# A hand-ordered mixer network: the same instructions in a new order, from a planner with another rule for GpSimd's single-column work

## The chip, the cores and the metric

The kernel runs on one core of one Trainium2 chip, as one program. The metric is the device time of that program in microseconds; the time before is the median of three runs. A core has TensorE (PE, matmuls into PSUM), VectorE (DVE), ScalarE (ACT), GpSimd (POOL) and SyncE (SP, which here only issues DMAs). Each engine works through its own instruction list strictly in order, and waits on semaphores for what other engines make.

## The reference

Two layers with shared weights, on x of 2048 rows and 512 columns in float32. Each layer is an attention A with a window of 8 keys at distance 2, and a mixer B:

```python
x = x + _A_ref(_layernorm(x), A_wqkv, A_wo)
x = x + _B_ref(_layernorm(x), B_w1, B_w2, B_w3, B_w4)
# and both once more

def _A_ref(x, wqkv, wo):            # 32 heads of 16, W = 8 keys at offsets 0, 2, .., 14 back
    q, k, v = split(x @ wqkv)
    logits = einsum("bhsd,bhswd->bhsw", q, k_window) * 16 ** -0.5
    logits = where(position >= 0, logits, -1e9)
    o = einsum("bhsw,bhswd->bhsd", softmax(logits), v_window)
    return o @ wo

def _B_ref(x, w1, w2, w3, w4):      # w1, w2: 512x512; w3: 512x1792; w4: 1792x512
    h = gelu(_layernorm(x) @ w1)
    hs = concatenate(h's four quarters of columns, shifted by +1, -1, +2, -2 rows) @ w2
    x1 = x + hs
    return x1 + gelu(_layernorm(x1) @ w3) @ w4
```

## The kernel before

Tiles are of 128 rows. A block is 512 rows (four tiles), and the two layers make eight blocks, numbered 0 to 7 (0 to 3 are the first layer's). A block goes through five stages: p1 (layernorm, x @ wqkv, results to DRAM), p2 (attention, read back from DRAM so that a window lies in one partition), p3 (wo, layernorm, w1, Gelu, shifted copies), p4 (w2, residual, layernorm) and p5 (w3, Gelu, w4, residual, in 14 chunks of 128 hidden columns). Stages of different blocks overlap freely.

A float32 product is made from fp16 pieces: each operand is scaled and split in a high and a low part, and three matmuls of 512 columns replace one. A group of 12 matmuls (4 row blocks times 3) is the usual unit on TensorE. Block 0 uses float32 matmuls, since its weights are not yet split; the splitting of the weights (`small_weight` for wo, w1, w2 and `big_pair` for chunks of w3 and w4: a Square with a running sum on ScalarE, a one-column matmul with `ones` that sums over partitions, a power on GpSimd, then the high and low parts) runs beside the first blocks.

What the engines do around the matmuls:

- ScalarE evicts PSUM, does Gelu and the exponential (two function tables, ACT_TABLE_LOAD between them), the Square sums of layernorm (`junk<-`), the normalizations and the high parts.
- VectorE does the attention: products of 128x2048 elements (`prod<-kv,q`, `prod<-kv,L`), their sums (`L<-prod`, `prod<-prod`, `o<-prod`), and low parts (SCALAR_TENSOR_TENSOR, TENSOR_TENSOR subtractions) and residual additions.
- GpSimd does the column work of layernorm, `power`: three instructions on single columns of the tile `small` (scale and add, power -0.5, the shift), written `small<-small`. It also takes some of VectorE's and ScalarE's wide work and the small shifted copies `h<-h` in p3.
- SyncE issues DMAs, the transposing ones too (`xt<-f`, `nT<-f`, `oT<-f`), which turn a normalized tile for the next matmul.

The order is not the program's. Each step is recorded as an operation with its alternatives (engine, expected duration, function), its reads and writes, and a place in one global order, from the table `PLACES`; the table `OTHER` names the operations that take their second alternative, another engine. `plan` sorts by place, hands out buffers of each kind (x, f32, mm for PSUM and so on) by its own expected times, and issues; a helper, `InOrder`, keeps every engine to that order. All instructions are issued through the helper, so the profile puts them all on line 338 (347 after the change), and they are told apart by their tiles. Where names differ between the two orders (`nT_168`, `nT_170`; `prod_206`, `prod_203`), they are buffers' numbers. Four buffers of 512 columns are quarters of the tile `prod0`, so a normalized tile can bear the name `prod`.

In the planner's model an operation has a class: "lock" is a VectorE instruction with two operands in SBUF, which shares a port with GpSimd. Before the change every GpSimd operation and every lock operation waits in the model for the one before it:

```python
if e == POOL or cls == "lock":
    begin = max(begin, port)
    port = begin + d
```

The steps that the prediction speaks of are `power` and `power_of` (columns), `sq_dev` (Square sums), `normed` (normalization), `turn_dma` (transposing DMA), `hi_of` and `rest` (parts of weights), the copies in `p3`, and the stages that call them.

Of the kernel before, what the change touches and what calls it, by code (L numbers as in the profile page):

```python
# [218 lines left out]
class Graph:  # L219
# [3 lines left out]
    def __call__(self, key, alts, r=(), w=(), after=(), xfer=0.0, late=0.0):  # L223
# [34 lines left out]
        return o  # L258


LAT, LAT_PE, LAT_SP, LAT_DMA, LEAD, TABLE, COLD = 0.06, 0.4, 0.15, 1.5, 0.85, 1.3, 1.0
TAIL = (0.165, 0.085, 0.115, 0.0, 0.0)
FREE = (6.5, 1.0, 0.72, 1.2, 0.72)
LANES = 8
BY_DMA = {"p1": 1, "p2": 1, "p3": 1, "p4": 1}


def plan(ops, slots):


    free, latest = list(FREE), {}
# [1163 lines left out]
```

## Time and profile before

| | |
|---|---|
| median of three runs | 1144.0 us |
| lowest and highest run | 1142.68 and 1894.58 us |
| the profiled execution | 1145.03 us |
| its span, first to last instruction | 1143.2 us |
| busy: TensorE / VectorE / ScalarE / GpSimd | 98% / 75% / 54% / 37% |
| granted TensorE clock, mean | 0.997 |
| moved by DMA | 206.37 MB, 181 GB/s |

One of the three runs took 1894.58 us, far from the other two. "Busy" counts an engine's own work; TensorE's weight loads (PEld) overlap its matmuls. A group's row ends with busy time, mean duration of one in ns, and the idle time just before its instructions with what ended it. An "issue" is time without a wait that the profile shows.

### The profile page before, as it was taken

To read this page: it belongs to the slowest core of one execution; us is meant where nothing else is said; L and a number is where in the kernel's file an instruction comes from. 1 tells how busy PE (TensorE), PEld (TensorE's weight loads), DVE (VectorE), ACT (ScalarE), POOL (GpSimd) and SP (SyncE) were. 2 spreads that over 40 slices of the span, in tenths; PEclk is the share of its full clock that TensorE was granted. 3 is DMA by queue.
4 is the path that set the end of the run, shared out by engine and by line. 5 is a ranking of instruction groups with operands and counts; after the bars stand their busy time and mean duration, and the time that the engine had idled before them with its cause. 6 is when DMAs were issued, how large, how long until landed. Compare 5 with 4: busy or idle time off the path is not lost.

```text
span 1143.2 us, 15112 instructions
## 1 busy us (share of the span) xinstructions
PE 1124.1 (98%) x5190; PEld 532.4 (47%) x5190; DVE 862.6 (75%) x919; ACT 618.6 (54%) x1089; POOL 417.9 (37%) x596
## 2 busy tenths in 40 slices
PE   8989999999999999999999999999999999999998
PEld 6544445554444444444444444444444444444554
DVE  4989899997899998988888888378986888323212
ACT  4766785247863565464654565354555554535321
POOL 4342364125652571135534353252324342322000
PEclk9999999999999999999999999999999999999999
DMA  6988989997989669974679756596687865524322
GB/s 175 217 205 215 223 216 259 256 238 182 265 234 222 162 161 211 244 187 121 161 182 230 192 136 166 128 237 177 154 206 166 199 168 158 113 75 112 100 88 79
DMA packets 249165, 206.37 MB, mean 181 GB/s; under 512 B 131032, under 2 KB 192472, under 8 KB 249088
## 3 DMA queue, kind: packets, MB, share of 16 engines
q1 hardware_dynamic: 247472, 203.63, 72.3%
q10 hardware_dynamic: 1616, 1.77, 0.5%
q8 instruction: 41, 0.67, 0.2%
q14 instruction: 36, 0.29, 0.1%
HBM read 132.64 MB, written 37.87 MB: 149 GB/s over the span
## 4 chain that ended last, share of the span: by engine, by line
PE 60%; ACT 2%; DVE 1%; issue 1%; POOL 1%; POOLq 0%; DVEq 0%; ACTq 0%
PE mm L338 42%; PE acc L338 18%; POOL small L338 1%; ACT f L338 1%; DVE L L338 0%; DVE prod L338 0%; ACT junk L338 0%; DVE f L338 0%; ACT L338 0%; ACT g L338 0%; ACT mm L338 0%; POOL f L338 0%; DVE x L338 0%; POOL o L338 0%; DVE h L338 0%
## 5 line engine op out<-in xcount | busy, mean ns | idle before, releaser
L338 PE MATMUL acc<-w,g 128*128 128x512 f16 (+1 forms) x1260 | 307.3, 394 | 0.0
L338 PE MATMUL mm<-nT,w 128*128 128x512 f16 (+1 forms) x1288 | 301.7, 389 | 0.8 <-ACT f L338 0.8
L338 PE MATMUL mm<-wq_hl,xt 128*128 128x512 f16 x1008 | 226.8, 381 | 3.2 <-DMA xt<-f 2.3
L338 ACT ACTIVATE mm<-mm,s_w 128x512 f32<-128x512 f32 (+1 forms) x144 | 89.7, 628 | 195.0 <-PE mm L338 194.7
L338 PEld LDWEIGHTS <-w 128*128 128x128 f16 x1344 | 125.2, 98 | 142.2 <-issue 1.0
L338 PEld LDWEIGHTS <-g 128*128 128x128 f16 x1176 | 114.7, 98 | 137.5
L338 DVE TENSOR_TENSOR prod<-kv,L 128x2048 f32<-128x2048 f32 x64 | 148.7, 2325 | 13.6 <-POOL o L338 12.2
L338 PEld LDWEIGHTS <-xt 128*128 128x128 f16 x1008 | 98.8, 98 | 122.5 <-issue 4.8
L338 DVE TENSOR_REDUCE L<-prod 128x128 f32<-128x2048 f32 x64 | 146.2, 2284 | 1.2
L338 POOL TENSOR_SCALAR small<-small 128x1 f32<-128x1 f32 (+1 forms) x200 | 88.8, 444 | 137.8 <-ACT junk L338 123.8
L338 DVE TENSOR_TENSOR prod<-kv,q 128x2048 f32<-128x2048 f32 x58 | 134.3, 2316 | 3.7 <-DMA q<-q_d 1.9
L338 DVE TENSOR_TENSOR prod<-prod 128x512 f32<-128x512 f32 (+2 forms) x109 | 111.5, 1026 | 2.7
L338 POOL TENSOR_TENSOR g<-f,g 128x512 f16<-128x512 f32 x39 | 54.8, 1409 | 117.8 <-ACT g L338 69.2
L338 DVE SCALAR_TENSOR_TENSOR g<-mm,c_g,g 128x512 f16<-128x512 f32 x56 | 41.5, 745 | 63.7 <-ACT g L338 63.7
L338 PE MATMUL mm<-w_hl,h 128*128 128x512 f16 x384 | 85.7, 379 | 1.1 <-POOL h L338 1.1
L338 PE MATMUL mm<-nT,w_hl 128*128 128x512 f16 x384 | 86.5, 379 | 0.0
L338 POOL TENSOR_TENSOR small<-small,nhalf 128x1 f32<-128x1 f32 (+1 forms) x104 | 72.3, 695 | 8.7
L338 PE MATMUL mm<-wo_hl,oT 128*128 128x512 f16 x336 | 74.3, 379 | 0.0
L338 POOL TENSOR_TENSOR prod<-prod 128x512 f32<-128x512 f32 (+1 forms) x24 | 30.5, 1271 | 105.9 <-DVE prod L338 99.4
L338 ACT ACTIVATE ev<-mm,s_kv 128x512 f32<-128x512 f32 x56 | 38.1, 681 | 54.8 <-PE mm L338 40.0
L338 ACT ACTIVATE g<-mm,c_g 128x512 f16<-128x512 f32 x98 | 66.6, 684 | 1.9
L338 PEld LDWEIGHTS <-oT 128*128 128x128 f16 x426 | 41.5, 98 | 49.0 <-issue 0.6
(188 smaller groups left out, 1217.8 us busy)
## 6 DMA issues: line engine op xcount, KB each, us to landing
w<-w SPq DMA_DIRECT2D x196, 256.0 KB
kv<-kv_d SPq DMA_DIRECT2D x112, 352.0 KB
w<-in_B_w_dram SPq DMA_DIRECT2D x56, 256.0 KB
kv_d<-ev SPq DMA_DIRECT2D x112, 128.0 KB
q_d<-ev SPq DMA_DIRECT2D x28, 256.0 KB
w<-g SPq DMA_DIRECT2D x28, 256.0 KB
q<-q_d SPq DMA_DIRECT2D x28, 256.0 KB
x<-x SPq DMA_DIRECT2D x26, 256.0 KB
```

The source lines that it names most:

```text
L338: i = f(*a, **k).ins
```

## The change

The planner's model of the shared port changes, and with it the two tables. GpSimd's column operations (`power`, `power_of`'s power, and the four-column chain of p3) get the class "tiny". In the new model GpSimd still waits for a running lock operation, up to `GRANT` before its end; a lock operation waits only for wide GpSimd work (`wide`), not for tiny; and what needs a tiny operation's result waits another `HELD`. The latency to TensorE goes from 0.4 to 0.35, and some expected durations on GpSimd are new. The functions that make the instructions stay as they are; `PLACES` is another order, and `OTHER` moves some operations: GpSimd issues 36 instructions more, VectorE 12 and ScalarE 16 fewer (accumulator reads and the like not counted). TensorE's instructions are the same in number.

```diff
 PLACES = [int(k) for k in """
-15 29 72 33 3 148 0 1 6 5 19 12 8 13 7 21 40 58 20 45 2 4 14 16
+40 41 58 128 94 96 0 1 4 5 12 13 11 9 10 26 53 31 39 28 2 3 15 16
...
 OTHER = {int(k): 1 for k in """
-27 37 100 101 104 107 116 178 181 187 226 235 256 277 304 361 366 396 421 422 425 465 483 566
+27 32 37 102 103 106 114 118 120 126 140 158 177 178 181 183 187 201 205 225 228 229 231 232
...
-LAT, LAT_PE, LAT_SP, LAT_DMA, LEAD, TABLE, COLD = 0.06, 0.4, 0.15, 1.5, 0.85, 1.3, 1.0
+LAT, LAT_PE, LAT_SP, LAT_DMA, LEAD, TABLE, COLD = 0.06, 0.35, 0.15, 1.5, 0.85, 1.3, 1.0
 TAIL = (0.165, 0.085, 0.115, 0.0, 0.0)
 FREE = (6.5, 1.0, 0.72, 1.2, 0.72)
 LANES = 8
+GRANT, HELD = 0.14, 0.6
...
-    dma_free, port, table, order = 0.0, 0.0, None, []
+    dma_free, port, wide, table, order = 0.0, 0.0, 0.0, None, []
...
-            if e == POOL or cls == "lock":
-                begin = max(begin, port)
+            if e == POOL:
+                if begin < port:
+                    begin = max(begin, port - GRANT)
+                if cls != "tiny":
+                    wide = begin + d - GRANT
+            elif cls == "lock":
+                begin = max(begin, wide)
                 port = begin + d
             if e == PE and begin - free[PE] > COLD and begin > 20.0:
                 d += min(begin - free[PE] - COLD, 2.5)
             o.end = begin + d + (TAIL[PE] if e == PE else 0.0)
             free[e] = o.end - TAIL[e]
+            if cls == "tiny":
+                o.end += HELD
...
-    def gp(key, d, fn, r, w, after=()):
-        return op(key, [(POOL, d, fn, None)], r, w, after)
+    def gp(key, d, fn, r, w, after=(), cls=None):
+        return op(key, [(POOL, d, fn, cls)], r, w, after)
...
-        gp(key, 1.24, fn, [(ss, j), (tot, k)], [(ve, i), (r, i), (nb, i)])
+        gp(key, 1.24, fn, [(ss, j), (tot, k)], [(ve, i), (r, i), (nb, i)], cls="tiny")
```

Three places of the new order. The first is ScalarE at the Square of w2 (`w_hl,ss_w_152`), some 60 us in; `ev` are evictions of the first layer's qkv results for block 1. Before:

```order
L338 ACTIVATE wo_hl<-nT_200,inv_wo 128x1024
L338 ACTIVATE ev_208<-mm_66,s_kv 128x512
L338 ACTIVATE junk,ss_p_146<-w_188 128x512
L338 ACTIVATE junk,ss_p_146<-w_192 128x512
L338 ACTIVATE w_hl,ss_w_152<-nT_168 128x2048
L338 ACTIVATE ev_209<-mm_68,s_kv 128x512
L338 ACTIVATE ev_165<-mm_70,s_q 128x512
```

and now:

```order
L347 ACTIVATE wo_hl<-nT_195,inv_wo 128x1024
L347 ACTIVATE ev_208<-mm_70,s_kv 128x512
L347 ACTIVATE ev_209<-mm_66,s_q 128x512
L347 ACTIVATE w_hl,ss_w_152<-nT_170 128x2048
L347 ACTIVATE ev_194<-mm_68,s_kv 128x512
```

Two evictions stand ahead of the Square, where one stood, and two Squares of `big_pair` (`ss_p_146`) no longer stand between.

The second is ScalarE at the Squares of `big_pair` 1 (`ss_p_141`), some 279 us in; `f_182<-x_194` (before) and `f_198<-x_205` (now) are the normalization of a tile of block 4, which waits for GpSimd's columns. Before:

```order
L338 ACTIVATE junk,small<-x_194,small 128x512
L338 ACTIVATE junk,small<-x_185,small 128x512
L338 ACTIVATE junk,ss_p_141<-w_192 128x512
L338 ACTIVATE f_182<-x_194,small 128x512
L338 ACTIVATE junk,ss_p_141<-w_193 128x512
L338 ACTIVATE f_204<-f_182 128x512
```

and now:

```order
L347 ACTIVATE junk,small<-x_205,small 128x512
L347 ACTIVATE junk,small<-x_186,small 128x512
L347 ACTIVATE junk,ss_p_141<-w_184 128x512
L347 ACTIVATE junk,ss_p_141<-w_165 128x512
L347 ACTIVATE f_198<-x_205,small 128x512
L347 ACTIVATE prod_203<-f_198 128x512
```

Both Squares now stand ahead of the normalization.

The third is GpSimd some 540 us in, where block 3's shifted copies (`h_175<-h_184`, now `h_180<-h_181`) stand among p4's columns and wide work. Before:

```order
L338 TENSOR_SCALAR small<-small 128x1
L338 TENSOR_TENSOR small<-small,nhalf 128x1
L338 TENSOR_SCALAR small<-small 128x1
L338 MEMSET h_175 128x2x2
L338 TENSOR_TENSOR f_171<-f_173,f_171 128x512
L338 TENSOR_SCALAR f_204<-prod_206,small 128x512
L338 TENSOR_SCALAR small<-small 128x1
L338 TENSOR_TENSOR small<-small,nhalf 128x1
L338 TENSOR_SCALAR small<-small 128x1
L338 COPY h_175<-h_184 128x2
L338 COPY h_175<-h_184 128x2x2
```

and now:

```order
L347 COPY h_180<-h_181 128x2x2
L347 TENSOR_SCALAR small<-small 128x1
L347 TENSOR_TENSOR small<-small,nhalf 128x1
L347 TENSOR_SCALAR small<-small 128x1 x2
L347 TENSOR_TENSOR small<-small,nhalf 128x1
L347 TENSOR_SCALAR small<-small 128x1
L347 COPY h_180<-h_181 128x2
L347 TENSOR_TENSOR x_192<-x_192,prod_203 128x512
L347 TENSOR_TENSOR f_177<-f_168,f_177 128x512
```

One copy stands ahead of both column chains and one right behind them; the wide work follows.

More of the change, by code (lines that the diff above doesn't have):

```diff
@@ L556, in power_of @@
         p = inv.t[:, :m] if inv.kind is None and not isinstance(inv.t, tuple) else inv.t
-        gp(key, 1.03, lambda: G.tensor_tensor(p, f2.t[:, :m], nhalf[:, :m], ALU.pow), [f2], [inv])
+        gp(key, 1.03, lambda: G.tensor_tensor(p, f2.t[:, :m], nhalf[:, :m], ALU.pow), [f2], [inv], cls="tiny")
         def cut():
@@ L1094, in p2_unit @@
                 dve(kd + 0.01, 1.215, lambda f=add4: f(V), [], [pr], lock=True)
-                op(kd + 0.01, [(DVE, 0.692, lambda f=add2: f(V), "lock"), (POOL, 1.2, lambda f=add2: f(G), None)], [], [pr])
+                op(kd + 0.01, [(DVE, 0.692, lambda f=add2: f(V), "lock"), (POOL, 1.27, lambda f=add2: f(G), None)], [], [pr])
                 added = op(kd + 0.01, [(DVE, 0.425, lambda f=add1: f(V), "lock"),
-                                       (POOL, 0.65, lambda f=add1: f(G), None)], [pr], [(o, i)])
+                                       (POOL, 0.73, lambda f=add1: f(G), None)], [pr], [(o, i)])
             if n == 0 and qt == 3:
@@ L1171, in p3 @@
         tiles = list(range(NT))
-        gp(key + 0.2, 1.93, r1_of, [(ss, tiles), (sums, tiles)], [(r1, tiles), ve1, (nb1, tiles)])
+        gp(key + 0.2, 1.93, r1_of, [(ss, tiles), (sums, tiles)], [(r1, tiles), ve1, (nb1, tiles)], cls="tiny")
         h = hs[n] = Buf("h")
@@ L1202, in p3 @@
                 e = slice(8, 9 + (g == 2))
-                gp(key, 0.49, lambda g=g, k=k, e=e: G.tensor_copy(
+                gp(key, 0.39, lambda g=g, k=k, e=e: G.tensor_copy(
                     hview(h)[:, :, g, k, 1:64], hview(h)[:, :, g, e, 0:63]), own, [(h, ("L", g))])
                 if hprev is None:
-                    gp(key, 0.25, lambda g=g, k=k: G.memset(hview(h)[:, :, g, k, 0:1], 0.0),
+                    gp(key, 0.2, lambda g=g, k=k: G.memset(hview(h)[:, :, g, k, 0:1], 0.0),
                        own, [(h, ("Le", g))])
                 else:
-                    gp(key, 0.25, lambda g=g, k=k, e=e: G.tensor_copy(
+                    gp(key, 0.2, lambda g=g, k=k, e=e: G.tensor_copy(
                         hview(h)[:, :, g, k, 0:1], hview(hprev)[:, :, g, e, 63:64]),
@@ L1214, in p3 @@
                 e = slice(0, 1 + (g == 3))
-                gp(key, 0.49, lambda g=g, k=k, e=e: G.tensor_copy(
+                gp(key, 0.39, lambda g=g, k=k, e=e: G.tensor_copy(
                     hview(h)[:, :, g, k, 0:63], hview(h)[:, :, g, e, 1:64]), own, [(h, ("R", g))])
                 if hprev is not None:
-                    gp(key, 0.25, lambda g=g, k=k, e=e: G.tensor_copy(
+                    gp(key, 0.2, lambda g=g, k=k, e=e: G.tensor_copy(
                         hview(hprev)[:, :, g, k, 63:64], hview(h)[:, :, g, e, 0:1]),
@@ L1221, in p3 @@
                 if b == NB - 1:
-                    gp(key, 0.25, lambda g=g, k=k: G.memset(hview(h)[:, :, g, k, 63:64], 0.0),
+                    gp(key, 0.2, lambda g=g, k=k: G.memset(hview(h)[:, :, g, k, 63:64], 0.0),
                        own, [(h, ("Re", g))])
```

283 rows, old and new, of tables (OTHER, PLACES) are left out of this document.

## The prediction, made before the result was known

> **What bounds the kernel now.** I read the busy shares of the page first, then what TensorE waits for, then TensorE's own instructions around its longest waits, and last the two or three engines behind each of these waits.
>
> The busy line of the page, and the list of TensorE's waits (us in total, times, longest):
>
> ```profile
> PE 1124.1 (98%) x5190; PEld 532.4 (47%) x5190; DVE 862.6 (75%) x919; ACT 618.6 (54%) x1089; POOL 417.9 (37%) x596
> ...
> PE mm L338 <- ACT f L338: 3.1, 4, 1.4
> PE mm L338 <- POOL f L338: 2.3, 2, 1.7
> PE mm L338 <- DMA xt<-f: 2.3, 2, 1.6
> PE mm L338 <- ACT ev L338: 2.1, 2, 1.9
> PE mm L338 <- ACT junk L338: 1.3, 1, 1.3
> PE mm L338 <- POOL h L338: 1.1, 1, 1.1
> PE mm L338 <- DVE nhalf L338: 1.0, 1, 1.0
> PE mm L338 <- DVE h L338: 0.7, 1, 0.7
> PE mm L338 <- DMA nT<-in_A_wqkv_dram: 0.5, 1, 0.5
> ```
>
> TensorE is the bound: of a span of 1143.2 us it is idle for 19.1. The listed waits add up to 14.4, of which 1.0 stands before its first matmul; the other 13.4 lie between matmuls. The rest, 4.7, is the end, after the last matmul. The change takes no matmul away, so it can only shorten these 13.4 us, and what follows from them. TensorE's instructions at the larger ones (start, us, what, and in brackets the idle time before it and what ended it), with a full-speed group from the chain of waits ahead of them, and then three stretches (length, busy us of PE, PEld, DVE, ACT, POOL, then the granted clock):
>
> ```profile
> 465.22 2.59 PE acc L338 x12
> ...
> 18.43 0.66 PE L338 MATMUL mm<-ident,f 128*128 128x128 f32 x4 [1.67 <-POOL f L338]
> ...
> 61.93 0.38 PE L338 MATMUL mm<-ss_w,ones 128*128 128x1 f32 x2 [1.90 <-ACT ev L338]
> 62.50 4.75 PE L338 MATMUL mm<-wq_hl,xt 128*128 128x512 f16 x14 [0.19 <-ACT ev L338]
> ...
> 84.63 1.69 PE L338 MATMUL mm<-wq_hl,xt 128*128 128x512 f16 x7 [1.62 <-DMA xt<-f]
> ...
> 279.76 0.39 PE L338 MATMUL mm<-ss_p,ones 128*128 128x4 f32 x2 [1.29 <-ACT junk L338]
> ...
> 546.61 1.69 PE L338 MATMUL mm<-w_hl,h 128*128 128x512 f16 x7 [1.11 <-POOL h L338]
> ...
> 573.45 1.89 PE L338 MATMUL mm<-nT,w 128*128 128x512 f16 x8 [0.76 <-ACT f L338]
> ...
> 1136.65 1.89 PE L338 MATMUL mm<-w,oT 128*128 128x512 f16 x8
> ...
> 60.00:68.00 8.00, 5.91 (x22) 2.48 (x22) 4.43 (x6) 7.27 (x19) 0.00 (x0) 0.79 0.74 217
> ...
> 413.00:546.00 133.00, 132.29 (x612) 59.72 (x611) 117.35 (x114) 72.19 (x117) 50.39 (x74) 1.00 0.82 191
> ...
> 574.00:1139.00 565.00, 564.54 (x2741) 260.58 (x2738) 360.28 (x373) 271.15 (x451) 175.34 (x257) 1.00 0.61 153
> ```
>
> A group of 12 matmuls at full speed takes 2.59 us, 0.216 each. The 14 behind the wait at 61.93 took 4.75: 14 x 0.216, and the 0.16 that a last matmul adds (the 8 at 573.45 take 1.89), make 3.18, so 1.57 us went to the lowered clock (0.79 in that stretch). After 574 TensorE is idle for 0.5 us in 565. All that can be won therefore lies before 574: 13.4 of waits and 1.6 of clock, 15.0 us or 1.3% of the time. What measurement of this kernel can tell from no change is about 2%, or 22.9 us. The forecast is inside that whichever way the details fall, unless something new and large comes in.
>
> **What the change rests on.** The planner now lets GpSimd's single-column work stand beside VectorE's two-operand instructions. Three pairs of a GpSimd and a VectorE instruction show what this kernel does there:
>
> ```profile
> 537.11 2.31 POOL L338 TENSOR_SCALAR small<-small 128x1 f32<-128x1 f32 x1 [1.39 <-ACT junk L338]
> ...
> 537.09 2.28 DVE L338 TENSOR_TENSOR prod<-kv,q 128x2048 f32<-128x2048 f32 x1
> ...
> 304.02 0.55 POOL L338 TENSOR_TENSOR small<-small,nhalf 128x1 f32<-128x1 f32 x1
> ...
> 304.12 0.69 DVE L338 TENSOR_TENSOR f<-prod,f 128x512 f16<-128x512 f32 x1 [0.51 <-ACT f L338]
> ...
> 620.17 1.16 POOL L338 TENSOR_TENSOR prod<-f,prod 128x512 f16<-128x512 f32 x1
> ...
> 620.41 3.06 DVE L338 TENSOR_TENSOR prod<-kv,q 128x2048 f32<-128x2048 f32 x1
> ```
>
> A single column on GpSimd that meets a running two-operand instruction waits for its end (2.31 us). The reverse does not hold: at 304.12 VectorE starts inside a GpSimd column of 0.55 us and takes 0.69. Only a wide GpSimd instruction holds VectorE up: 3.06 us at 620.41 against 2.28, which is 0.78 us, the part of the 1.16 that was left. So the new rule describes the trace, and the old one made the planner keep VectorE waiting where nothing waits. The Trainium skill (SBUF — State Buffer, "Who interferes with whom") has it otherwise: of a VectorE instruction with two SBUF inputs and a GpSimd instruction, whichever starts first holds the shared port pair for the whole instruction and the other fully blocks. The rows agree for the wide instruction and for the column that comes second, not for the column that comes first.
>
> **The change part by part.** No instruction changes its shape, and moved work costs what it cost before. The terms are the waits of TensorE that the new order touches, and new ones.
>
> (a) The wait at 61.93. ScalarE's instructions before it, and SyncE's:
>
> ```profile
> 59.30 1.91 ACT L338 ACTIVATE w_hl<-nT 128x2048 bf16<-128x2048 f32 x1 [4.46 <-DMA nT<-in_B_w_dram]
> 61.21 0.67 ACT L338 ACTIVATE ev<-mm,s_kv 128x512 f32<-128x512 f32 x1
> 61.78 0.68 ACT L338 ACTIVATE ev<-mm,s_q 128x512 f32<-128x512 f32 x1
> ...
> 43.14 1.85 SPq L338 DMA_TRANSPOSE xt<-f  x1
> ...
> 49.10 0.48 SPq L338 DMA_DIRECT2D nT<-in_B_w_dram  x1
> ```
>
> ScalarE stands at the Square of a small weight until the weight has landed, and two evictions queue behind it, whose PSUM buffers TensorE needs; the matmul at 61.93 also needs the Square's sum. In the new order both evictions stand ahead of the Square, and on SyncE three issues (x in two halves, one shift) stand between the transpose and this load, where six stood; those six took 49.10 - 43.14 - 1.85 = 4.1 us, so three less are 2 us. Landing 2 us sooner, the Square ends at 59.2, and TensorE is free at 60.0 (61.93 - 1.90). What goes is 1.90 + 0.19 of waits and 1.57 of clock, 3.7 us. If the landing doesn't move, the Square still ends at 61.2, 1.3 of the 1.9 stays and the clock may fall as well: the term is 0.6 to 3.7. I take 3.7, since both causes are moved.
>
> (b) The waits at 84.63, 279.76, 546.61 and 573.45. In each an engine's fixed order puts what TensorE needs behind something that it doesn't:
>
> ```profile
> 68.42 2.71 POOL L338 TENSOR_TENSOR o<-prod 128x256 f32<-128x256 f32 x1 [9.98 <-DVE prod L338]
> ...
> 72.20 0.19 POOL L338 TENSOR_SCALAR small<-small 128x1 f32<-128x1 f32 x1
> ...
> 278.28 0.81 ACT L338 ACTIVATE f<-x,small 128x512 f32<-128x512 f32 x1 [1.75 <-POOL small L338]
> 279.00 0.61 ACT L338 ACTIVATE junk<-w 128x512 bf16<-128x512 f32 x1
> ...
> 543.75 0.76 POOL L338 TENSOR_SCALAR f<-prod,small 128x512 f32<-128x512 f32 x1
> ...
> 568.87 1.28 ACT L338 ACT_TABLE_LOAD   x1
> ```
>
> At 84.63 the transposed tile is late because GpSimd's columns for it (72.20) stand behind an addition that first waited 9.98 us and then ran 2.71; now they stand ahead of it: 1.62. At 279 the Square at 279.00, whose sum TensorE waits for, stands behind a normalization that waits 1.75 us for a column; now it stands ahead: 1.29. At 546 two small copies of h stand on GpSimd behind a wide normalization (543.75, now ScalarE's), a wide subtraction and a column chain; now one copy precedes the first column chain and the other follows the second, with the wide work behind both: 1.11. At 573 ScalarE goes to the exponential's table and back (568.87 is the way back) shortly before TensorE needs four evictions; the exponential's VectorE input now has some four instructions of about 0.7 us (like 304.12) fewer ahead of it, three of them GpSimd's now, so both loads come sooner: 0.76. Together 4.8 us. Each could stay, if what follows is late for its own reasons: 0 to 4.8. Three of the four are plain changes of place in a queue, and I take 4.8. That exposes what comes next, which is (d).
>
> (c) What I leave at zero. In the first 20 us the chain is GpSimd's normalization of the fourth tile (1.67 at 18.43). GpSimd's memsets now stand behind it, but one group of matmuls that covered part of the wait moves behind it too. Taken at 0, bounds -0.5 and +1.7. The same for the other wait on xt (2.3 - 1.62 = 0.7), for what is left of those on ACT f after the first 20 us (about 0.9) and for the 0.7 on DVE h, 2.3 together: the chains that feed TensorE there keep their distance. The end (4.7 us from 1138.5 to 1143.2) has the same instructions in nearly the same order: 0.
>
> (d) New waits. Some thirty stretches of TensorE's order change, by one to five groups of 2.59 us, and most other rows of the four engines move too. Margins shrink in places: in the last block the w2 group of the second tile (mm<-w_hl,h) now stands one group after the last w1 group instead of three, which leaves 2.59 us for Gelu, copy and VectorE's subtraction. Two ScalarE passes like the evictions in (a), 0.67 and 0.68, and the subtraction, by its group
>
> ```profile
> L338 DVE SCALAR_TENSOR_TENSOR h<-mm,c_h,h 128x512 f16<-128x512 f32 x32 | 23.1, 745 | 17.7 <-ACT h L338 17.7
> ```
>
> make 2.1, and the hand-overs fill the rest. The trace of before can't show which of these fall short. Its own order has nine waits after 20 us, 9.1 us in all, about one each. I take three to four new ones of that size, 3.5 us; bounds 0 and 9.1.
>
> Sum: 3.7 + 4.8 - 3.5 = 5.0. The span goes from 1143.2 to 1138.2. The profiled execution took 1145.0, 1.8 more than its span, and the median of the runs is 1144.0, 1.0 under that: 1138.2 + 1.8 - 1.0 = **1139.0 us**.
>
> **The rivals.**
>
> *The gains come back as other waits (25%).* An order made for a model has waits where the chip departs from it; the old one had 9.1 us, and the new one may have as many. The time stays at 1142 to 1145. For it speaks that VectorE is full where most waits are (117.35 of 133 us before 546); against it that the waits in (a) and (b) have named causes that the order moves.
>
> *The wide work on GpSimd holds VectorE up: slower (15%).* GpSimd gets 36 more instructions, none of them a column, and each can hold VectorE up as at 620.41, by 0.78 us. 36 times 0.78 is 28 us of VectorE at worst. VectorE has 15.7 us free in the 133 before 546, and at that rate 60 between 68 and 574, so I let a third reach TensorE: 9 us, without any gain from (b), since these chains run over VectorE. 1144 + 9 - 3.7 = 1149 us. It decides when VectorE's idle time before 574 falls to the size of TensorE's waits.
>
> *GpSimd's columns block VectorE after all (2%).* The order has 104 column chains on GpSimd; with 0.19 (72.20) for the first and the last instruction and 0.55 (304.02) for the power each holds VectorE for up to 0.9 us, 97 in all. Half of them stand before 574, and half of that as lost gives 1144 + 24 = 1168. The row at 304.12 speaks against it. This is the Trainium skill's rule in SBUF — State Buffer ("Who interferes with whom"), taken without exception for small instructions.
>
> *All goes (8%).* No new wait at all: 1139.0 - 3.5 = 1135.5, and with (c) at its best (1.7 and 2.3) 1131.5.
>
> The forecast itself, 1136 to 1142, has the remaining 50%.
>
> **How the numbers follow.** The range 1131 to 1149 holds the forecast, the case in which all goes, the gains that come back and the centre of the slower case. Left out are half of the slower case, the blocked columns and small tails of the others: under 2 in 10. Faster by over 2% would mean under 1121, below the 1143.2 - 15.0 + 0.8 = 1129 that is left when nothing waits: 1%. Slower by over 2% is the blocked columns and the far end of the wide work: 4%. Within 2%: 95%.
>
> **What would show it.** TensorE's list of waits should fall from 14.4 to about 10, without entries above 1.0 after 60 us, and the clock in the stretch around 60 us should be 1.00. (b) is wrong where the same matmuls (ss_p behind the second block's second w1 group, the fourth block's last w2 group) still carry idle time. The wide rival would show as VectorE's two-operand groups with longer means than now (2.28 for the product at 537.09) and more busy time than 862.6. If a column holds VectorE up, instructions like that at 304.12 take over a microsecond. The forecast is wrong if TensorE's busy time itself differs from 1124 by more than 2 us, or if new waits pass 9 us.

## The result, and the profile after

The changed kernel takes 1153.8 us (median of four runs). The kernel before takes 1144.0 us, the median of its runs without the one slow run of 1894.58 us. The ratio is 1.0086, with a 95% interval of 1.0064 to 1.0109: within 2%, but slower, and outside the range of 1131 to 1149. The profiled execution has a span of 1151.6 us.

The busy line of the changed kernel's page, and its two groups of single-column instructions on GpSimd:

```profile
PE 1127.5 (98%) x5190; PEld 533.0 (46%) x5190; DVE 873.2 (76%) x906; ACT 609.5 (53%) x1074; POOL 503.0 (44%) x632
...
L347 POOL TENSOR_SCALAR small<-small 128x1 f32<-128x1 f32 (+1 forms) x200 | 115.8, 579 | 127.3 <-ACT junk L347 112.1
...
L347 POOL TENSOR_TENSOR small<-small,nhalf 128x1 f32<-128x1 f32 (+1 forms) x104 | 87.7, 843 | 8.7
```

The same two groups of the kernel before:

```profile
L338 POOL TENSOR_SCALAR small<-small 128x1 f32<-128x1 f32 (+1 forms) x200 | 88.8, 444 | 137.8 <-ACT junk L338 123.8
...
L338 POOL TENSOR_TENSOR small<-small,nhalf 128x1 f32<-128x1 f32 (+1 forms) x104 | 72.3, 695 | 8.7
```

GpSimd is busy for 503.0 us instead of 417.9, with only 36 instructions more. Exactly as many column instructions as before take 203.5 us instead of 161.1, so 42.4 of the 85.1 us are columns that take longer. TensorE's waits in the changed kernel (us in total, times, longest):

```profile
PE mm L347 <- DVE h L347: 4.0, 3, 2.2
PE mm L347 <- DMA xt<-f: 3.1, 3, 1.5
PE mm L347 <- ACT junk L347: 2.8, 2, 2.1
PE mm L347 <- ACT ev L347: 2.1, 2, 2.0
PE acc L347 <- ACT g L347: 1.7, 1, 1.7
PE mm L347 <- DVE nhalf L347: 1.0, 1, 1.0
PE mm L347 <- ACT f L347: 0.9, 1, 0.9
PE mm L347 <- POOL f L347: 0.9, 1, 0.9
PE mm L347 <- DMA nT<-prod: 0.8, 1, 0.8
PE mm L347 <- DVE mx L347: 0.7, 1, 0.7
PE acc L347 <- POOL g L347: 0.6, 1, 0.6
```

With two more of 0.4 and 0.3 they sum to 19.3 us, against 14.4. The first 20 us hold 3.2 of them (5.2 before), and the rest of the program 16.1 (9.2 before). Four stretches of the changed kernel (length, busy us of PE, PEld, DVE, ACT, POOL, the granted clock, then DMA):

```profile
60.00:68.00 8.00, 8.00 (x36) 4.13 (x35) 7.93 (x12) 3.37 (x11) 1.42 (x2) 1.00 0.93 231
145.70:148.90 3.20, 3.20 (x9) 1.17 (x8) 2.00 (x2) 0.00 (x0) 2.93 (x5) 0.52 0.82 222
280.00:413.00 133.00, 128.43 (x587) 57.62 (x586) 114.17 (x124) 75.53 (x129) 67.98 (x74) 0.99 0.78 206
309.00:313.00 4.00, 4.00 (x13) 1.56 (x14) 4.00 (x3) 3.44 (x8) 3.59 (x5) 0.57 1.12 268
```

The wait at 61.93 and the low clock behind it are gone (first row). New are waits between 105 and 569 us; from 280 to 413 alone TensorE is idle for 4.57 us (third row), where it was for 0.47 before. New are also two stretches at a granted clock of 0.52 and 0.57 behind two of these waits; they cost 3.20 x 0.48 + 4.00 x 0.43 = 3.3 us.

One of these waits, followed back. TensorE at 144.22 in the changed kernel, and ScalarE, GpSimd and VectorE in the 8 us before it (start, us, engine, operation, and in brackets the idle time before it and its releaser):

```profile
137.45 2.29 DVE L347 TENSOR_TENSOR prod<-kv,q 128x2048 f32<-128x2048 f32 x1
137.62 2.52 POOL L347 TENSOR_TENSOR small<-small,nhalf 128x1 f32<-128x1 f32 x1
...
139.66 1.28 DVE L347 SCALAR_TENSOR_TENSOR w_hl<-h,inv_w,w_hl 128x1024 f16<-128x1024 f32 x1
140.25 0.82 POOL L347 TENSOR_SCALAR small<-small 128x1 f32<-128x1 f32 x1
...
141.10 1.52 ACT L347 ACTIVATE prod<-x,small 128x512 f32<-128x512 f32 x2 [2.73 <-POOL small L347]
142.53 1.06 ACT L347 ACTIVATE nT<-mm 128x512 f16<-128x512 f32 x2
143.48 0.68 ACT L347 ACTIVATE ev<-mm,s_kv 128x512 f32<-128x512 f32 x1
...
144.22 0.66 PE L347 MATMUL mm<-ident,prod 128*128 128x128 f32 x4 [1.96 <-ACT ev L347]
```

One chain of three columns meets two VectorE instructions in turn. Its power waits for the product that began 0.17 us before it (2.52 us in all), and its last column for VectorE's next two-operand instruction (0.82). ScalarE stands for 2.73 us at the normalization that reads them, and an eviction behind it frees TensorE's buffer late. TensorE's wait of 2.23 us at 419.51 has such a chain behind it too. Here the first two columns wait, and the third hardly (0.33 us):

```profile
408.61 2.29 DVE L347 TENSOR_TENSOR prod<-kv,L 128x2048 f32<-128x2048 f32 x1 [0.18 <-POOL o L347]
409.37 1.58 POOL L347 TENSOR_SCALAR small<-small 128x1 f32<-128x1 f32 x1 [0.80 <-ACT junk L347]
...
410.94 1.95 DVE L347 TENSOR_TENSOR prod<-prod 128x1024 f32<-128x1024 f32 x2
411.04 1.55 POOL L347 TENSOR_TENSOR small<-small,nhalf 128x1 f32<-128x1 f32 x1
412.69 0.33 POOL L347 TENSOR_SCALAR small<-small 128x1 f32<-128x1 f32 x1
...
413.05 0.81 ACT L347 ACTIVATE f<-x,small 128x512 f32<-128x512 f32 x1 [3.77 <-POOL small L347]
```

The tile that this normalization makes reaches TensorE at 418.40. The low part of h, which ends the wait, starts on VectorE at 418.71, behind a product of 128x2048. So the chain is not the whole of this wait.

Over all chains of columns, counted from the first to the last instruction of each, 35 of 104 take over 3 us; before, 14 did. Of the 92 chains of three, 50 have a column that takes over 0.15 us longer than it takes unhindered (0.19, 0.55 and 0.265 us), and 17 have two or three such columns; before, it was 38 and 10. All that the columns take beyond these durations is 88 us, and was 52. All three wait in only four chains, as at 446.47 (2.17, 0.88 and 0.76 us). What ScalarE's normalizations wait for them, in the changed kernel and then in the kernel before:

```profile
ACT f L347 <- POOL small L347: 40.1, 26, 4.4
...
ACT prod L347 <- POOL small L347: 19.8, 10, 4.1
```

```profile
ACT f L338 <- POOL small L338: 25.6, 17, 3.2
...
ACT prod L338 <- POOL small L338: 5.6, 4, 2.4
```

That is 59.9 us instead of 31.2. No row here shows VectorE held up by a column. In the changed kernel it starts inside one of 0.55 us and takes its usual 0.69:

```profile
262.82 0.55 POOL L347 TENSOR_TENSOR small<-small,nhalf 128x1 f32<-128x1 f32 x1
...
263.04 0.69 DVE L347 TENSOR_TENSOR f<-f,f 128x512 f16<-128x512 f32 x1 [0.35 <-ACT f L347]
```

The same holds wherever a VectorE TENSOR_TENSOR starts inside a column that itself waits for nothing: in the 19 cases of the changed kernel that can be compared, none takes over 0.03 us more than the median of the same instruction alone.

Three theories follow from this. **Theory 1:** the chains are the cause; the new model counts one wait for a chain of three instructions, and on the chip each of them can wait anew. **Theory 2:** GpSimd's wide work holds VectorE up (the prediction's slower rival). VectorE is busy 10.6 us longer; its larger groups of two-operand instructions take 22.6 us more beside wide GpSimd work than at the median of the same instruction alone, against 10.0 before (beside columns nothing in either). **Theory 3:** the places themselves are worse, whatever the port does.

### The profile page after: what moved, and what is told of

Its sections match the earlier page's. It is cut to its first block, busy times and chain, and to the rows that moved or that the text cites. A ratio compares the mean times of both kernels' runs of the same rounds, so it can differ in the third digit from the quotient of the medians.

```text
span 1151.6 us, 15079 instructions
## 1 busy us (share of the span) xinstructions
PE 1127.5 (98%) x5190; PEld 533.0 (46%) x5190; DVE 873.2 (76%) x906; ACT 609.5 (53%) x1074; POOL 503.0 (44%) x632
## 4 chain that ended last, share of the span: by engine, by line
PE 54%; POOL 8%; issue 5%; DVE 5%; ACT 5%; DMA 1%; SPq 1%; POOLq 0%; ACTq 0%; DVEq 0%
PE mm L347 38%; PE acc L347 16%; POOL small L347 4%; DVE prod L347 2%; ACT f L347 2%; POOL g L347 1%; DVE L L347 1%; ACT junk L347 1%; ACT L347 1%; ACT prod L347 1%; SPq L347 1%; POOL prod L347 0%; ACT mm L347 0%; DVE x L347 0%; POOL h L347 0%
## 5 line engine op out<-in xcount | busy, mean ns | idle before, releaser
L347 PE MATMUL mm<-wq_hl,xt 128*128 128x512 f16 x1008 | 229.2, 383 | 7.5 <-DVE h L347 4.0
L347 POOL TENSOR_SCALAR small<-small 128x1 f32<-128x1 f32 (+1 forms) x200 | 115.8, 579 | 127.3 <-ACT junk L347 112.1
L347 DVE TENSOR_TENSOR prod<-kv,q 128x2048 f32<-128x2048 f32 x58 | 139.5, 2406 | 3.3 <-DMA kv<-kv_d 2.0
L347 DVE TENSOR_TENSOR prod<-prod 128x1024 f32<-128x1024 f32 (+2 forms) x114 | 121.3, 1065 | 4.0 <-ACT prod L347 1.0
L347 POOL TENSOR_TENSOR g<-f,g 128x512 f16<-128x512 f32 x31 | 45.5, 1470 | 106.0 <-ACT f L347 60.7
L347 POOL TENSOR_TENSOR small<-small,nhalf 128x1 f32<-128x1 f32 (+1 forms) x104 | 87.7, 843 | 8.7
L347 PEld LDWEIGHTS <-w_hl 128*128 128x128 f16 x384 | 37.4, 98 | 47.6 <-issue 3.3
```

Source lines behind the costliest of these rows:

```text
L347: i = f(*a, **k).ins
```

## The experiments

**One short column per chain, in both orders.** In `power`, in the changed kernel and in the kernel before (the tile `small` is set to zero first, since most of its columns are no longer written):

```diff
+V.memset(small, 0.0)
...
-G.tensor_scalar(ve.t[:, s], ss.t[:, j:j + 1], c1, c2, ALU.mult, ALU.add)
-G.tensor_tensor(r.t[:, s], ve.t[:, s], nhalf[:, :1], ALU.pow)
-G.tensor_scalar(nb.t[:, s], tot.t[:, k:k + 1], r.t[:, s], c, ALU.mult, ALU.mult)
+G.tensor_scalar(r.t[:, s], ss.t[:, j:j + 1], SN / D ** 3, SN, ALU.mult, ALU.min)
```

> The changed kernel in its own order, but each per-tile column chain (power) is one short instruction, r = min(ss*k, 1024), instead of three (scale and add, power, shift). It leaves out the power, the epsilon and the shift, so the normalized values are not those of the reference; all other instructions, engines and places stay. Theory 1 (chains): in the changed kernel's trace 35 of 104 chains take over 3 us (14 before), since each of the three column instructions waits anew for a running two-operand VectorE instruction, and TensorE's waits at 144, 309 and 419 us follow such chains; with one instruction most of the 16 us lost after 130 us goes: 1138 to 1144 us. Theory 2 (wide work): GpSimd's wide instructions hold VectorE up by 22.6 us instead of 10.0 (durations over the median of the same instruction alone); this stays: 1150 to 1154. Theory 3 (the places themselves: what stands behind what in the queues, whatever the port does): 1150 to 1154.

> The kernel before, with the same edit (one short column instruction per chain; power, epsilon and shift are left out). Its own waits (61.93, 84.63, 279.76, 413, 546, 573 us) come from queues and loads more than from chains, so by all theories it stays near its time, 1139 to 1144. What tells them apart is the distance to the changed kernel with the same edit: theory 1 within 3 us of each other, theories 2 and 3 the changed kernel 7 to 10 us longer, as without the edit.

Measured: 1138.2 us for the changed order (0.9951 of the kernel before, 0.9936 to 0.9967), 1138.3 for the order before (0.9951, 0.9938 to 0.9965). The 9.8 us between the two kernels are gone. Of the changed kernel the edit takes 15.6 us, of the kernel before 5.7, to just below the 1139 to 1144 that all theories had for it: the old order lost time to its chains too. Theories 2 and 3 are out as the main cause: the wide work and the places are as they were.

**One long column per chain.** The short column above might have won by its length alone. Here it is a power over three columns, in place of the same three instructions:

```diff
...
+G.tensor_tensor(r.three[:, 3 * i:3 * i + 3], v.to_broadcast([P, 3]), power3, ALU.pow)
```

> The changed kernel, each per-tile column chain one instruction again, but a long one: a power over three columns, which by the trace's 0.55 us for one column and 1.02 us for four should take about 0.86 us, against 0.19 + 0.55 + 0.27 = 1.01 us for the three instructions without waits. It leaves out the scale and epsilon and the shift, and takes another exponent. Theory 1a (each of the three instructions waits anew for VectorE): the number of waits counts, not the work, and the time is near that with one short instruction (1138.2): 1138 to 1142. Theory 1b (the chain is only too long): with 0.86 of 1.01 us still there most of the loss stays: 1149 to 1153.

Measured: 1137.6 us (0.9946, 0.9927 to 0.9965). Its busy line, the group, TensorE's largest waits and ScalarE's waits for the columns:

```profile
PE 1123.3 (99%) x5190; PEld 532.7 (47%) x5190; DVE 872.9 (77%) x908; ACT 609.1 (54%) x1074; POOL 451.3 (40%) x440
...
L347 POOL TENSOR_TENSOR small<-small,power 128x3 f32<-128x3 f32 x92 | 117.7, 1283 | 138.4 <-ACT junk L347 138.4
```

```profile
PE mm L347 <- DMA nT<-in_A_wqkv_dram: 2.0, 1, 2.0
PE mm L347 <- DVE h L347: 2.0, 3, 1.2
...
ACT f L347 <- POOL small L347: 19.1, 16, 2.4
...
ACT prod L347 <- POOL small L347: 7.4, 5, 2.4
```

A chain's columns take 117.7 / 92 = 1.28 us, waits included, where the three took 203.5 / 104 = 1.96. TensorE's waits after 20 us fall from 16.1 to 3.3. The work of a chain is nearly all still there, and the whole loss is gone (the time is 0.4 us below the range for 1a): what counts is that three instructions can wait, and not how long they work. VectorE is as busy as in the changed kernel (872.9 us against 873.2). Counted over the groups of 20 and more two-operand instructions, it loses 23.5 us beside wide work here, 24.4 in the changed kernel and 10.4 in the kernel before (22.6 and 10.0 above are over other groups). So with one column per chain, what the wide work costs VectorE doesn't reach TensorE.

**The old choice of engines in the new places.** `OTHER` of the kernel before with `PLACES` and model of the changed one:

```diff
-OTHER = (that of the changed kernel)
+OTHER = (that of the kernel before)
```

> The changed kernel's places (PLACES) and model with the kernel before's choice of engines (OTHER): 91 operations return to their first engine and 62 take the second one again, so GpSimd has its old 596 instructions. Theory 2: the hold-ups of VectorE fall back towards 10 us and with them the loss, while the 7 us won in the first 100 us stay: 1137 to 1144. Theory 1: the chains stand where they stood, and VectorE has more two-operand instructions for them to wait for: 1152 to 1160. Theory 3: 1150 to 1156.

Measured: 1177.4 us (1.0311, 1.0279 to 1.0343), beyond every expectation. What TensorE waits for there:

```profile
PE mm L346 <- DVE h L346: 6.7, 5, 3.0
PE mm L346 <- DVE mx L346: 6.7, 3, 4.5
PE mm L346 <- DMA xt<-f: 4.3, 3, 3.3
```

Three quarters of these three lines, the largest of 38.7 us of waits in all, are waits on VectorE, which has the work back at places that were made without it. The run says little on theory 2: by the same count VectorE still loses 19.7 us beside wide work, not the 10 that the expectation reckoned with. What it shows is that places and engines belong together, and one can't be judged by exchanging it alone.

**Two columns per chain, then one, with all the work done.** ScalarE does the first column behind its Square sum (`after_ve`); then the shift as well (`after_ve2`), so that GpSimd keeps only the power (but for one tile, which it normalizes itself):

```diff
+A.activation(ve.t[:, s], ss.t[:, s], AF.Copy, scale=c1, bias=c2)        # behind the Square
-G.tensor_scalar(ve.t[:, s], ss.t[:, j:j + 1], c1, c2, ALU.mult, ALU.add)
# after_ve2 also:
+A.activation(nb.t[:, s], tot.t[:, k:k + 1], AF.Copy, scale=C0)           # behind the Square
+A.activation(nb.t[:, s], nb.t[:, s], AF.Copy, scale=r.t[:, s])           # ahead of the normalization
-G.tensor_scalar(nb.t[:, s], tot.t[:, k:k + 1], r.t[:, s], c, ALU.mult, ALU.mult)
```

> The changed kernel with two column instructions per chain on GpSimd instead of three: the first (scale and add epsilon) is done by ScalarE, right behind the Square sum that it reads, as one more 128x1 instruction; the result is the reference's. If each column instruction waits anew, a third of the chain's waits goes and the time falls from 1153.8 by about a third of the 15.7 us that went with two instructions and their work: 1147 to 1150. If ScalarE's added instruction (about 100 times some 0.2 us, 20 us of an engine that is 53% busy) stands in the way: 1153 to 1158. If chains are not the cause: 1152 to 1155.

> The changed kernel with one column instruction per chain left on GpSimd, the power of 0.55 us; ScalarE does the first (scale and add, behind the Square) and the shift (two 128x1 instructions, one behind the Square, one ahead of the normalization). The result is the reference's. Waits per chain on GpSimd: three gave 1153.8, two gave 1144.4; with the two one-instruction kernels at 1137.6 and 1138.2, one should give 1138 to 1141 if the number of waits decides; 1144 to 1148 if ScalarE's some 60 us of added column work now costs as much as it brings.

Measured: 1144.4 us for two columns (0.9999, 0.9983 to 1.0015), 1146.1 for one (1.0023, 1.0010 to 1.0035). The first step wins 9.4 us, 60% of what one short column won and more than any of its expectations, and makes the changed order as fast as the kernel before. The second wins nothing more. Its ScalarE columns by group:

```profile
L347 ACT ACTIVATE small<-small 128x1 f32<-128x1 f32 x275 | 51.7, 225 | 17.5 <-POOL small L347 14.6
```

They add 51.7 us to ScalarE, and a shift now stands in ScalarE's queue ahead of each normalization there. That this is what takes the further gain back fits the row and the second half of the expectation, but no run here separates it.

**The first 100 us of one order, the rest of the other.** The places are joined: the first 380 operations of the changed order, then what is left in the order before, each part with its own engines. The model, which hands out the buffers, is the changed one throughout.

> The changed kernel's order and engines for its first 380 operations (to about 100 us on TensorE), the order and engines of the kernel before for all the rest. Against the work done, the changed kernel is 7.1 us ahead of the kernel before at that point (14.5 us lost there by the kernel before, 7.4 by the changed one) and loses 15.5 us to it between there and 600 us. If the two parts are independent (theories 1 to 3 alike): 1144 - 7 = 1137. If the lead is used up because the early start meets later loads or full buffers: 1141 to 1145. If the loss comes from what the first 100 us leave behind (buffers, queues): 1148 or more.

Measured: 1141.9 us (0.9985, 0.9972 to 0.9997). A gain, but 2.1 us where independent parts would give 7. Where the two orders meet TensorE waits for a transposed tile:

```profile
106.28 1.04 PE L346 MATMUL mm<-wq_hl,xt 128*128 128x512 f16 x4 [1.55 <-DMA xt<-f]
```

A part of the lead is used up, as the second expectation had it. The loss of the changed order lies behind its first 100 us, since it isn't here.

**The prediction's terms (b) by themselves.** In the kernel before, four moves in `PLACES` and nothing else:

```diff
+big_pair.1: second Square directly behind the first (ScalarE)
+p3.3: two copies of h directly behind the memset of h (GpSimd)
+p2_unit.3: reduction L<-prod behind one low part of h (VectorE)
+p2_unit.4, p5.3: exponential and its input earlier, one normalization behind Gelu (VectorE, ScalarE)
```

> The kernel before with four local moves and nothing else of the change: (1) the second Square of big_pair 1 right behind the first on ScalarE, ahead of the normalization that waits for a column (the wait at 279.76); (2) two copies of h on GpSimd right behind the memset of h, ahead of wide work and a column chain (546.61); (3) the reduction L<-prod on VectorE behind one low part of h instead of ahead of it (413.22); (4) the exponential and its VectorE input ahead of two Squares, and Gelu's first instruction ahead of a normalization (573.45). This tries the terms (b) of the prediction in an order without its new waits. If each wait goes and nothing new comes: 1.45 + 1.27 + 0.86 + 0.92 = 4.5 us, 1139.5. If what stands behind each is as late: 1143 to 1145.

Measured: 1141.5 us (0.9973, 0.9955 to 0.9990), a gain of 1.1 to 5.1 us; the 2.6 of the medians lies between the two expectations. In its trace TensorE's waits after 20 us are 3.5 instead of 9.2, and none is left at the four places; one of 0.75 is new, at 549.51, behind the third. Of the 5.7 us of difference 2.1 are the wait at 61.93, which the moves don't touch (the last experiment is about it). So the three waits of (b) among them were what the prediction took them for, and they can be removed in an order without the new ones.

**All that helps.** The join at 493 operations (131 us, again with the changed model) with the four moves behind it, then with two columns per chain, and with one:

> The changed kernel's order and engines for its first 493 operations (to about 131 us on TensorE), the order and engines of the kernel before for the rest, and there the four local moves. The changed kernel leads by 5.4 us at that point; 5.4 + 4.5 = 9.9: 1134 if both hold. With the lead partly used up, as where the orders were joined at 100 us (2.1 us won instead of 7.1), 1137 to 1140. 1144 or more if both fail.

> The joined order with the four moves, with two column instructions per chain on GpSimd and one on ScalarE. Between the kernel without the edit (1138.6) and the one with a single column on GpSimd: 1135 to 1138.

> The joined order with the four moves (1138.6), with the same edit: one column instruction per chain on GpSimd, two more and one on ScalarE. Its order has fewer chains that TensorE waits for (2.3 us of waits on xt, 2.0 on ScalarE's f, in all some 8 us after 20 us). If chains stand behind those: 1133 to 1136. If what is left are loads and evictions: 1138 to 1140.

Measured: 1138.6 us (0.9954, 0.9938 to 0.9970); with two columns 1139.6 (0.9956, 0.9941 to 0.9970); with one 1143.5 (1.0002, 0.9988 to 1.0016). The first is as the partly used lead had it; the other two are above every expectation. The joined order beats both kernels, by 0.5% and 1.3%. In it the columns aren't worth moving any more: TensorE's waits after 20 us are 5.5 without that edit.

**The kernel before once more.**

> The kernel before, unchanged, a second profiled execution. The run with the four moves showed no wait at 61.93 us, although nothing near it was moved, and its start was 2 us later. If that wait and the start differ from one execution to the next, they differ here too, and the prediction's term (a) rests on one execution; if this trace has 1.9 us of wait and the lowered clock there again, the moves' other buffers took it away.

One execution, 1146.8 us. The first 24 us of the kernel before as it was first profiled, then the first 24 us and the stretch around 62 us of the second execution, in the same columns as above, and then TensorE and ScalarE at the places in question:

```profile
0.00:24.00 24.00, 18.70 (x114) 15.71 (x115) 7.88 (x21) 10.69 (x27) 11.66 (x41) 1.00 0.63 175
...
0.00:24.00 24.00, 19.06 (x101) 15.48 (x102) 7.51 (x19) 9.52 (x23) 11.87 (x41) 0.93 0.60 175
56.00:68.00 12.00, 12.00 (x56) 6.16 (x55) 11.04 (x11) 9.11 (x24) 1.28 (x1) 1.00 1.02 196
```

```profile
19.35 0.66 PE L338 MATMUL mm<-ident,f 128*128 128x128 f32 x4 [3.00 <-POOL f L338]
...
59.07 1.91 ACT L338 ACTIVATE w_hl<-nT 128x2048 bf16<-128x2048 f32 x1 [1.82 <-DMA nT<-in_B_w_dram]
...
62.46 0.28 PE L338 MATMUL mm<-ss_w,ones 128*128 128x1 f32 x2
```

There is no wait at 62 us, and the clock there is 1.00. The Square of w2 starts at 59.07, and started at 59.30 before. But at the start the normalization of the fourth tile ended its wait at 19.35 instead of 18.43 (3.00 us of wait instead of 1.67), and the lowered clock now follows this wait: 0.93 over the first 24 us instead of 1.00, which is 24 x 0.07 = 1.7 us. So TensorE came to the matmul only at 62.46, when the sum was there. Much of what was lost at 62 us in the first execution is lost at the start in the second. The four waits of (b) are there again, 2.49 at 84.03, 1.29 at 280.27, 1.11 at 548.33 and 0.75 at 575.16: these belong to the order, though the size of the first does not.

## Why the prediction was wrong, point by point

**What bounds the kernel** held: TensorE's work is the same, and the 8.4 us of span are 5.0 of idle time (24.1 against 19.1) and 3.4 of busy time (1127.5 against 1124.1), of which 3.3 - 1.6 = 1.7 is the lowered clock. The other 1.7 is not traced to a row. That a change under 2% can't be told from none did not hold: the interval of the result, 1.0064 to 1.0109, is clear of 1.

**What the change rests on** is where it failed. The pairs were read rightly, one by one: a column waits for a running two-operand instruction, VectorE doesn't wait for a column. (Of the wide instruction at 620.17 not 0.78 but 0.92 us was left at 620.41; 0.78 is the hold-up.) But "the new rule describes the trace" doesn't follow. The rule lets an operation wait once, and `power` is three instructions; while the first has waited and run, VectorE can have started its next. The row at 537.11 is the wait of one instruction of three, and the prediction drew from such rows only what VectorE no longer waits for; what the columns would then wait for VectorE got no term in the sum. The Trainium skill (SBUF — State Buffer, "Who interferes with whom" and "Summary: rules for kernel authors") says that a VectorE instruction with two SBUF inputs contends with a GpSimd instruction that reads SBUF, and that the second to issue is blocked until the first finishes. Taken per instruction, the trace agrees with it for columns that come second (2.52 and 0.82 us in one chain), and not for a VectorE instruction that comes second to a column (0.69 at 263.04, no longer than alone).

**(a)**, -3.7: gone as said, with the clock. w2's Square ends at 55.59 in the changed kernel, well before the 59.2 that was worked out for it. But the term rests on one execution. In the second one of the kernel before the wait wasn't there; the Square ended at 61.2 in the first and 60.98 in the second, and the matmul stood at 61.93 and 62.46. TensorE was held up once, with the lowered clock behind it, by the load in the first and at the start in the second; the new order moves both.

**(b)**, -4.8: three of the four waits are gone. The one at 84.63 (1.62, and 2.49 in the second execution) has shrunk to 0.55 at 77.61, ahead of the same matmul, so the term was -4.2. The four moves show that three of them can go without the rest of the change.

**(c)**, 0: the waits of the first 20 us fell from 5.2 to 3.2, so this term was -2.0, just past the gain of 1.7 that was its bound for the start; since the start differs between executions of one kernel, not all of it need be the order's. Of the 2.3 us of other waits that (c) left as they were, that on h at 413.22 grew from 0.69 to 2.23 ahead of the same matmul (now at 419.51), and the others are gone: together -0.1.

**(d)**, +3.5, bounds 0 to 9.1: the term of the sum that was mis-sized. Of the 16.1 us of waits after 20 us, 0.55 and 2.23 stand at old places, so 13.3 are new, and 3.3 of lowered clock come with them: 16.6. With one column per chain only 3.3 us of all the waits after 20 us are left, so most of this term is the price of the chains. The upper bound took the old order's waits as a measure of the new one. That couldn't bound it: the old model made VectorE's instructions and the chains yield to each other, and in an order from a model that doesn't, more chains meet VectorE (50 of 92 with a column that waits, instead of 38). The chains were priced at nothing, by the 0.19 and 0.55 of columns that met no one, although the page had them at 161.1 us for 104, or 1.55 each.

The sum: -3.7 - 4.2 - 2.0 - 0.1 + 16.6 = +6.6, and with the untraced 1.7 of busy time 8.3 of the +8.4.

**The rivals.** "The gains come back as other waits" was right in kind and stopped at the size of the old waits. "Wide work holds VectorE up" named a real effect (22.6 us against 10.0, VectorE at 873.2 us) and the right side of the result, but by luck, for the mechanism was another: with one column per chain the same wide work costs nothing at TensorE. "Columns block VectorE" is out. "All goes" is what the one-column kernels show, 1137.6 and 1138.2, without the columns' full work.

**What would show it** did: the list of waits rose instead of falling to 10, with entries above 1.0 after 60 us, busy time differs by over 2 us, and new waits pass 9 us. The clock around 60 us is 1.00, as forecast.

## What to carry to other kernels

Where one engine's instruction waits for the end of another's, price the waiting engine's work by instruction, not by operation: three small instructions in a row can wait two or three times, each for a long one. A group's mean well over its shortest member (0.44 against 0.19 us) is the sign of it, and the consumer's wait (ScalarE on the columns) its price. And when a re-made order is worse in one part and better in another, join the two orders where they agree: the join tells where the loss lies, and may be the best of the three.

## What the runs showed of the hardware that I had not expected

- Each short GpSimd instruction can wait anew for a running two-operand VectorE instruction: 2.17, 0.88 and 0.76 us in one chain of three (446.47), where 0.19, 0.55 and 0.265 are unhindered. One column instruction of three elements per partition in their place made the kernel 16.2 us shorter.
- VectorE's hold-ups by wide GpSimd work doubled (22.6 us instead of 10.0), and with one column per chain the time (1137.6 us) shows nothing of it.
- One wait at the start of one and the same kernel was 1.67 us in one execution and 3.00 in another. A stretch of lowered clock followed it in the second (0.93 over 24 us) and a later wait, at 61.93, in the first (0.79 over 8 us), and TensorE came to the same matmul at 61.93 and 62.46.
- A column takes ScalarE 0.225 us on average; the 275 of them, which overlap a little, keep it busy for 51.7 us. In the changed order moving one of three columns there took 9.4 us off the time, and moving a second one took off nothing more.
